# Two edits at the start of a fused attention and MLP kernel: which PSUM bank a score tile takes, and where the decay rows stand among the first loads

## The chip, the cores and the metric

The kernel runs on one core of one Trainium2 chip. The metric is the device time of one execution in microseconds. Three runs of the kernel before gave 341.88, 343.52 and 344.49 us (median 343.52). A profiled execution took 342.17 us, of which 340.5 us are the span that the profile shows; every time from the profile is counted from the start of that span.

## What is computed

Attention with a forget gate for 8 batches of 8 heads (sequence 576, head size 64), then an MLP over all 4608 tokens with an activation h - tanh(h):

```python
scores = scale * np.matmul(q, k.transpose(0, 1, 3, 2))
cum = np.cumsum(np.log(np.clip(f, 0.0001, 1.0)), axis=-1)
decay = cum[:, :, :, None] - cum[:, :, None, :]
scores = np.where(causal, -1000000000.0, scores + decay)
scores = scores - np.max(scores, axis=-1, keepdims=True)
attn = np.exp(scores)
attn = attn / (np.sum(attn, axis=-1, keepdims=True) + 1e-09)
x = np.matmul(attn, v)      # then tokens x 512
h = x @ w_in                # 512 -> 2048
out = (h - np.tanh(h)) @ w_out
```

## The kernel before

**Tiling.** The work is cut into 32 pairs of heads, four per batch; pair p is batch p // 4, heads 2c and 2c + 1 with c = p % 4. "Slot" in the change's short title is such a pair of batch 0, by its c. The scores of a pair are computed transposed (keys on partitions) in seven tiles (`TILES`, L337): three for each head, and between them tile 3 (`LAST`), which holds the last 64 keys of both heads and is only 128 columns wide. `scores` (L342) multiplies a tile on TensorE into a PSUM bank `ps` (L357), and ScalarE takes the exponential into SBUF (L366). In batch 0 the causal mask is a second matmul into the same bank (L360); from batch 1 on GpSimd masks after the exponential (L376). `values` (L387) multiplies with v into `av` (L394), and VectorE divides (L403 to L405).

**Decay.** It enters the matmul as three extra rows below the 64 of head size: rows `chi` and `clo` (high and low part of the cumulated logarithm) in KT, and `cq` in QT. For pair 0 these rows are computed in place (KS, QS). For the other heads of batch 0 they are copied by three small DMAs on GpSimd's queue, in `bulk` (L218, L220, L221); for later batches by SyncE (`load_aug`, L207). `chi`, `cq` and `clo` are ready at different times: `cq` from ScalarE (L583), `clo` from VectorE (L590).

**Transposes.** In the first two batches q and k come in with the sequence on partitions and are transposed by TensorE (`trans`, L303) and copied to QT and KT by VectorE or ScalarE (L314, L316). While pairs 0 to 3 run (`early`), the transposes go to the three banks `m0` to `m2`; from pair 4 on to the one bank of `ps_tr`. That bank also takes the unread warm-up matmuls of `unread` (L570) and, in batch 0, a third of the score tiles; the others alternate between the two banks of `ps_sc`. A bank is written again only when its last reader, the exponential, is through.

**Order.** All five engines run in the order in which the program is written (`manual_schedule`). `att_items` (L605) lists a pair's steps: scores of a tile, loads that go out at this tile (`LOADS`), transposes of the next pair, values of the pair before, and `turn` (L412), which turns an attention result into columns of XR, the MLP's input. From pair 4 on, steps of the MLP (`mlp1` L456, `mlp2_plain` L497, `mlp2` L521) are laid between them.

**Loads.** All loads from float32 inputs to float16 tiles are issued by GpSimd, one after the other; each of its loads waits until the load eight places ahead of it has landed. The order at the start is: q and k of heads 0 to 3 of batch 0, v for heads 0 and 1, then `bulk`: q and k of heads 4 to 7, the decay rows, v for heads 2 to 7 in four blocks (L131); then q and k of batch 1 in pieces, `win` in two halves (L226), four memsets (`last`, L600 to L603), v of batch 1, `wout` in two halves (L230), and q and k of batch 2 in one load of 576 KB each (L102).

Of the kernel before, what the change touches and what calls it, by code (L numbers as in the profile page):

```python
# [21 lines left out]
def kernel(  # L22
# [13 lines left out]
    B, H, S, D = q.shape  # L36
# [56 lines left out]
    qn, kn = ([t[0:S // NT6, :].rearrange("p (h n d) -> p h n d", h=H, n=NT6) for t in raw] for raw in (qraw, kraw))  # L93
# [7 lines left out]
    def load_qk(dst, src, b, h0, h1):  # L101
        nc.gpsimd.dma_start(  # L102
            out=dst[b % 2][:, h0:h1, :, :].rearrange("p h n d -> p h (n d)"),
            in_=src[b, h0:h1, :, :].rearrange("h (p n) d -> p h (n d)", n=NT6))
# [25 lines left out]
    def load_v_block(b, n, h0, h1):  # L130
        nc.gpsimd.dma_start(out=vn[b % 2][:, n, h0:h1, 0:D],  # L131
                            in_=v[b, h0:h1, n * P:(n + 1) * P, :].rearrange("h p d -> p h d"))
# [68 lines left out]
    def aug_rows(b):  # L201
        i, hs = b % 2, slice(b * H, (b + 1) * H)
        return [(KT[i][D:D + 1, :, 0:S], chi[hs, :]), (KT[i][D + 1:D + 2, :, 0:S], clo[hs, :]), (QT[i][D + 2:D + 3, :, :], cq[hs, :])]
# [10 lines left out]

    def bulk():
        (k_hi, chi_0), (k_lo, clo_0), (q_hi, cq_0) = aug_rows(0)
        load_qk(qn, q, 0, 4, H)
        nc.gpsimd.dma_start(out=k_hi, in_=chi_0)  # L218
        load_qk(kn, k, 0, 4, H)
        nc.gpsimd.dma_start(out=q_hi, in_=cq_0)  # L220
        nc.gpsimd.dma_start(out=k_lo, in_=clo_0)  # L221
        for n in range(NJ - 1):
            load_v_block(0, n, 2, H)

# [101 lines left out]
    def head_tiles(a):  # L326
        return [[(a, 0, 0, 512, 0)],
                [(a, 1, P, 448, 0), (a, 0, 512, 64, 448)],
                [(a, 2, 2 * P, 320, 0), (a, 3, 3 * P, 192, 320)]]
# [7 lines left out]
    TILES = head_tiles(0) + [[(0, 4, 512, 64, 64), (1, 4, 512, 64, 128)]] + head_tiles(1)  # L337
    LAST = 3
# [1 line left out]
             4: (0, 1, 1, P), 5: (0, 1, 1, P), 6: (0, 2, 320, P)}  # L340

    def scores(b, c, ti):  # L342
        if b == 0 and (((c - 1) * len(TILES) + ti) % 3 == 2 if c else ti == LAST):
            ps = ps_tr.tile([P, UW], FP32, tag="tr", name="ps")
        else:
            ps = ps_sc.tile([P, 512], FP32, tag="sc", name="ps")
        if ti == LAST:
            e = EL[(b * NPAIR + c) % 3]
        else:
            e = aex.tile([P, 512], FP16, tag="e", name="e")  # L350
        lo = min(x[4] for x in TILES[ti])
        hi = max(x[4] + x[3] for x in TILES[ti])
        kt, qt, rows = (KS, QS, NX) if b == 0 and c == 0 else (KT[b % 2], QT[b % 2], D + 3)
        for a, j, i0, n, col in TILES[ti]:
            h = 2 * c + a
            cut = min(P, n) if b == 0 and i0 == j * P else 0
            nc.tensor.matmul(out=ps[:, col:col + n], lhsT=kt[0:rows, h, j * P:(j + 1) * P],  # L357
                             rhs=qt[0:rows, h, i0:i0 + n], start=True, stop=cut == 0)
            if cut:
                nc.tensor.matmul(out=ps[:, col:col + cut], lhsT=id16, rhs=late[:, 0:cut],  # L360
                                 start=False, stop=True)
            for ib in range(j, NJ):
                w0 = min(ib * P, S - P)
                if i0 <= ib * P < i0 + n:
                    E[(b, c, a, j, ib)] = e[:, col + w0 - i0:col + w0 - i0 + P]
        nc.scalar.activation(out=e[:, lo:hi], in_=ps[:, lo:hi], func=AF.Exp, scale=qscale)  # L366
        if b == 0:
            return
        col, cp, step, wd = MASKS[ti]
        view = e[:, col:col + (cp - 1) * step + wd]  # L370
        if cp == 1:
            pat = [[1, wd]]
        else:
            view = bass.AP(view.tensor, view.offset, [list(view.ap[0]), [step, cp], [1, wd]])
            pat = [[0, cp], [1, wd]]
        nc.gpsimd.affine_select(out=view, in_=view, compare_op=ALU.is_ge, fill=0.0,  # L376
                                base=0, pattern=pat, channel_multiplier=-1)
# [198 lines left out]
    def start():  # L576
        def row_q(h, mul, add):
            nc.scalar.activation(out=QS[NH:NX, h, :], in_=cum[NH:NX, :], func=AF.Identity, bias=add[NH:NX, :], scale=mul[NH:NX, :])

        unread(47)  # L580
        row_q(0, mul_0, add_0)
        q_rest = trans(*pairs[0], qn, (QS,), True, "AAAA", True)
        nc.scalar.activation(out=cq, in_=cum[0:NH, :], func=AF.Copy, bias=-SHIFT * inv_qscale, scale=inv_qscale)  # L583
        unread(6)
        k_rest = trans(*pairs[0], kn, (KS,), True, "VVVV", True)
        unread(38)
        q_rest[0]()
        scores(*pairs[0], 0)
        unread(4)
        nc.vector.scalar_tensor_tensor(out=clo, in0=cum[0:NH, :], scalar=inv_qscale, in1=chi[0:NH, :], op0=ALU.mult, op1=ALU.subtract)  # L590
        nc.vector.tensor_copy(out=KS[NH:NX, 1, 0:S], in_=KS[NH:NX, 0, 0:S])
        for fn in k_rest:
            fn()
        scores(*pairs[0], 1)
        row_q(1, mul_1, add_1)
        unread(4)
        q_rest[1]()
# [7 lines left out]
    def att_items(p):  # L605
# [8 lines left out]
        for ti in range(len(TILES)):  # L614
            if here and (p > 0 or ti > 1):
                put(scores, *here, ti)
# [47 lines left out]
    at = 0  # L664
    start()
    bulk()
    for p in range(len(pairs) + 1):
        b, c = divmod(p, NPAIR)
# [54 lines left out]
```

## Time and profile before

| | |
|---|---|
| median of three runs | 343.52 us |
| profiled execution | 342.17 us |
| its span | 340.5 us |
| TensorE busy | 330.9 us, 97 % of the span |
| VectorE, ScalarE, GpSimd busy | 262.5, 235.1, 162.7 us |
| transfers issued by GpSimd | 18.39 MB, 92512 packets |

The page's second part cuts the span into 40 slices of 8.5 us; each digit is the busy share of an engine in tenths, and the last two rows give the mean busy share of the 16 DMA engines and what they moved:

```profile
PE   8798999999999999999999999999999999999995
DVE  8898887658887788677967886688668766966864
ACT  6897777888887886778677877787558842632630
POOL 8884846686657673776377547632322210000000
DMA  9999999999989999999999999990130023002003
GB/s 117 143 179 200 192 201 171 171 144 163 135 98 120 188 137 101 132 172 121 106 125 165 137 101 95 192 134 16 50 113 16 19 58 103 0 33 92 1 15 110
```

TensorE (PE) is full nearly everywhere; its gaps lie in the first slices and after its last matmul. The first slices hold batch 0, in which no MLP work fills the gaps yet. A busy share hides short waits, so the stretches, the waits and the order of single instructions must be read as well.

In the views that follow, a line gives start, length, engine, source line, operation, output and inputs; a bracket gives the idle time before it and what ended that. A "landing" is the time from the issue of a load to its end.

### The profile page before, as it was taken

The page shows a single profiled execution, that of the slowest core. Times are in us where ns is not written, and L with a number is a line of the kernel's source. Part 1 is how long each engine was busy: PE and PEld are TensorE (multiplying, and loading weights), DVE is VectorE, ACT ScalarE, POOL GpSimd, SP SyncE. Part 2 cuts the span into 40 slices and gives each one's busy share as a digit, 9 for nine tenths or more (in the row PEclk, how much of TensorE's full clock was granted, in tenths as well). Part 3 has the DMA queues.
Part 4 walks back from the last instruction along what each step waited for, and adds up shares of the span by engine and source line. Part 5 has one row for each costly group of instructions (what it writes and reads, how often), then busy time and mean ns, then how long its engine had stood idle before and what let it go on. Part 6 is the DMA issues. An engine that isn't in the chain of part 4 may idle for free.

```text
span 340.5 us, 8626 instructions
## 1 busy us (share of the span) xinstructions
PE 330.9 (97%) x3255; PEld 229.6 (67%) x3255; DVE 262.5 (77%) x516; ACT 235.1 (69%) x440; POOL 162.7 (48%) x321
## 2 busy tenths in 40 slices
PE   8798999999999999999999999999999999999995
PEld 7675555555588458855788888656875686486485
DVE  8898887658887788677967886688668766966864
ACT  6897777888887886778677877787558842632630
POOL 8884846686657673776377547632322210000000
PEclk9999999999999999999999999999999999999999
DMA  9999999999989999999999999990130023002003
GB/s 117 143 179 200 192 201 171 171 144 163 135 98 120 188 137 101 132 172 121 106 125 165 137 101 95 192 134 16 50 113 16 19 58 103 0 33 92 1 15 110
DMA packets 144941, 38.86 MB, mean 114 GB/s; under 512 B 128188, under 2 KB 143276, under 8 KB 144900
## 3 DMA queue, kind: packets, MB, share of 16 engines
q0 software_dynamic: 92512, 18.39, 72.9%
q1 hardware_dynamic: 52356, 19.88, 32.3%
q8 instruction: 25, 0.41, 0.5%
q14 instruction: 16, 0.13, 0.1%
q10 hardware_dynamic: 32, 0.06, 0.0%
HBM read 36.90 MB, written 9.44 MB: 136 GB/s over the span
## 4 chain that ended last, share of the span: by engine, by line
PE 82%; DMA 10%; POOL 6%; issue 1%; ACT 1%; DVE 0%; POOLq 0%
PE hps L456 33%; PE ops L521 29%; PE ps L357 10%; PE av L394 7%; DMA kn<-in_k_dram 6%; DMA win<-in_moe_w_in_dram 4%; PE ops L497 3%; POOL qn L102 1%; POOL vn L131 1%; POOL kn L102 1%; POOL vn L127 1%; PE t L303 1%; POOL vn L123 0%; ACT KT L314 0%; POOL win L226 0%
## 5 line engine op out<-in xcount | busy, mean ns | idle before, releaser
L456 PE MATMUL hps<-XR,win 128*128 128x512 f16 (+1 forms) x640 | 141.0, 357 | 0.3 <-ACT XR L426 0.2
L461 ACT ACTIVATE th<-hps 128x512 f32<-128x512 f32 x144 | 86.7, 602 | 55.2 <-PE hps L456 52.4
L467 DVE TENSOR_TENSOR gq<-hps,th 128x512 f16<-128x512 f32 x144 | 98.3, 688 | 25.0 <-ACT th L461 23.5
L366 ACT ACTIVATE e<-ps 128x512 f16<-128x512 f32 x192 | 110.3, 597 | 10.0 <-PE ps L357 6.6
L376 POOL TENSOR_SCALAR_AFFINE_SELECT e<-e 128x128 f16<-128x128 f16 x168 | 60.5, 362 | 69.5 <-ACT e L366 67.1
L456 PEld LDWEIGHTS <-win 128*128 128x128 f16 x640 | 57.7, 97 | 48.7 <-issue 0.7
L357 PE MATMUL ps<-QT,KT 67*128 67x512 f16 (+1 forms) x372 | 73.6, 276 | 1.8 <-DMA KT<-clo 1.0
L521 PEld LDWEIGHTS <-gq 128*128 128x128 f16 x640 | 60.3, 97 | 11.1
L521 PE MATMUL ops<-wout,gq 128*128 128x256 f16 x512 | 63.2, 272 | 0.0
L357 PEld LDWEIGHTS <-KT 67*128 67x128 f16 x372 | 35.3, 98 | 25.1 <-DVE KT L316 1.9
L394 PEld LDWEIGHTS <-e 128*128 128x128 f16 x896 | 32.3, 97 | 4.2
L394 PE MATMUL av<-vn,e 128*128 128x65 f16 x896 | 33.6, 193 | 0.0
L131 POOL DMA_DIRECT2D vn<-in_v_dram x32 | 28.0, 877 | 8.1 <-DMA win<-in_moe_w_in_dram 3.0
L521 PE MATMUL ops<-W,sq 128*128 128x256 f16 x256 | 31.2, 272 | 0.0
L405 DVE TENSOR_TENSOR xn<-av,rs 128x640 f16<-128x640 f32 x32 | 26.4, 825 | 1.1
L521 PEld LDWEIGHTS <-sq 128*128 128x128 f16 x256 | 24.1, 97 | 3.4
L376 POOL TENSOR_SCALAR_AFFINE_SELECT el<-el 128x128 f16<-128x128 f16 x28 | 9.3, 332 | 28.4 <-ACT el L366 28.0
L108 POOL DMA_DIRECT2D kn<-in_k_dram x25 | 21.2, 847 | 1.5 <-issue 1.3
L108 POOL DMA_DIRECT2D qn<-in_q_dram x25 | 21.2, 847 | 1.3 <-issue 0.9
L403 DVE TENSOR_SCALAR rs<-av 128x10 f32<-128x10 f32 x32 | 5.2, 162 | 18.9 <-PE av L394 17.8
L536 ACT ACTIVATE m<-ops 128x512 f32<-128x512 f32 x16 | 9.5, 596 | 10.9 <-PE ops L521 10.9
L316 DVE COPY QT<-t 64x576 f16<-64x576 f16 x18 | 14.4, 802 | 2.9 <-PE t L303 2.8
(93 smaller groups left out, 314.4 us busy)
## 6 DMA issues: line engine op xcount, KB each, us to landing
out_dram<-ost SPq DMA_DIRECT2D x34, 256.0 KB
vn<-in_v_dram POOLq DMA_DIRECT2D x24, 128.0 KB, 6.1
qn<-in_q_dram POOLq DMA_DIRECT2D x20, 128.0 KB, 5.0
kn<-in_k_dram POOLq DMA_DIRECT2D x20, 128.0 KB, 4.5
win<-in_moe_w_in_dram POOLq DMA_DIRECT2D x2, 1024.0 KB, 12.2
wout<-in_moe_w_out_dram POOLq DMA_DIRECT2D x2, 1024.0 KB, 14.6
XR<-xn SPq DMA_TRANSPOSE x56
vn<-in_v_dram POOLq DMA_DIRECT2D x12, 64.0 KB, 5.5
```

The lines of the kernel that those rows point to most:

```text
L108: nc.gpsimd.dma_start(out=dst[b % 2][0:pn, n, :].rearrange("p (h d) -> p h d", h=H), in_=src[b, :, n * P:n * P + pn, :].rearrange("h p d - ...
L131: nc.gpsimd.dma_start(out=vn[b % 2][:, n, h0:h1, 0:D], in_=v[b, h0:h1, n * P:(n + 1) * P, :].rearrange("h p d -> p h d"))
L316: nc.vector.tensor_copy(out=to, in_=of)
L357: nc.tensor.matmul(out=ps[:, col:col + n], lhsT=kt[0:rows, h, j * P:(j + 1) * P], rhs=qt[0:rows, h, i0:i0 + n], start=True, stop=cut == 0)
L366: nc.scalar.activation(out=e[:, lo:hi], in_=ps[:, lo:hi], func=AF.Exp, scale=qscale)
L376: nc.gpsimd.affine_select(out=view, in_=view, compare_op=ALU.is_ge, fill=0.0, base=0, pattern=pat, channel_multiplier=-1)
L394: nc.tensor.matmul(out=av[:, a, ib, :], lhsT=E.pop((b, c, a, j, ib)), rhs=vn[b % 2][:, j, 2 * c + a, 0:D + 1], start=(j == 0), stop=(j == ib))
L405: nc.vector.tensor_tensor(out=xn.rearrange("p i (a d) -> p a i d", a=2), in0=av[:, :, :, 0:D], in1=rs.to_broadcast([P, 2, NJ, D]), op=ALU. ...
L456: nc.tensor.matmul(out=hps[:, o:o + n], lhsT=win[:, ci, ft * P:(ft + 1) * P], rhs=XR[:, ci, t:t + n], start=(ci == 0), stop=(ci == NCH - 1))
L461: nc.scalar.activation(out=th, in_=hps, func=AF.Tanh, scale=-1.0)
L467: nc.vector.tensor_tensor(out=GQ[(u, i)][:, half, kt, :], in0=hps, in1=th, op=ALU.add)
L521: nc.tensor.matmul(out=ps[:, m, :], lhsT=LHS[lhs](u, kt // 4)[:, kt % 4, m * P:(m + 1) * P], rhs=rhs[:, kt, :], start=(fresh and (apart or ...
```

## The change

The first hunk reorders `bulk`. Before, q of heads 4 to 7 is one load, then the chi row, then k of heads 4 to 7 as one load, then the cq and the clo row. Afterwards q and k of heads 4 and 5 go out first, then the three rows, then q and k of heads 6 and 7; the blocks of v follow as before. The bytes are the same; two loads of 288 KB become four of 144 KB.

The second hunk changes which score tiles of pairs 1 to 3 of batch 0 take the transposes' bank: those whose running number (7 (c - 1) + tile) leaves the remainder 0 instead of 2 when divided by 3. Pair 1 had tiles 2 and 5 there and now has 0, 3 and 6; pair 2 had 1 and 4 and now has 2 and 5; pair 3 had 0, 3 and 6 and now has 1 and 4. Pair 0 (tile 3) is unchanged. The other tiles take the two banks of `ps_sc` in turn, and the order of instructions on TensorE, VectorE, ScalarE and SyncE stays the same.

```diff
     def bulk():
         (k_hi, chi_0), (k_lo, clo_0), (q_hi, cq_0) = aug_rows(0)
-        load_qk(qn, q, 0, 4, H)
+        load_qk(qn, q, 0, 4, 6)
+        load_qk(kn, k, 0, 4, 6)
         nc.gpsimd.dma_start(out=k_hi, in_=chi_0)
-        load_qk(kn, k, 0, 4, H)
         nc.gpsimd.dma_start(out=q_hi, in_=cq_0)
         nc.gpsimd.dma_start(out=k_lo, in_=clo_0)
+        load_qk(qn, q, 0, 6, H)
+        load_qk(kn, k, 0, 6, H)
         for n in range(NJ - 1):
             load_v_block(0, n, 2, H)
...
     def scores(b, c, ti):
-        if b == 0 and (((c - 1) * len(TILES) + ti) % 3 == 2 if c else ti == LAST):
+        if b == 0 and (((c - 1) * len(TILES) + ti) % 3 == 0 if c else ti == LAST):
             ps = ps_tr.tile([P, UW], FP32, tag="tr", name="ps")
```

## The prediction

> **What bounds the kernel now.** I read four views in this order: busy time by stretch, the chain of waits, TensorE's own idle times, then GpSimd's queue beside VectorE's. The first says where time can change at all (columns: stretch, its length, then busy us of TensorE, weight loads, VectorE, ScalarE, GpSimd, the clock, the DMA share, GB/s):
>
> ```profile
> 8.50:17.00 8.50, 6.46 (x97) 5.13 (x94) 6.85 (x12) 7.33 (x14) 7.33 (x12) 1.00 1.46 142
> 17.00:34.00 17.00, 15.42 (x247) 11.20 (x244) 15.53 (x28) 14.59 (x30) 11.34 (x19) 1.00 1.26 190
> 34.00:57.00 23.00, 22.12 (x195) 12.03 (x194) 20.01 (x33) 18.07 (x35) 14.88 (x31) 1.00 1.50 192
> 60.00:300.00 240.00, 239.96 (x2319) 166.01 (x2318) 183.79 (x361) 174.65 (x330) 119.53 (x243) 1.00 1.13 110
> ```
>
> From 60 to 300 us TensorE is busy for 239.96 of 240.00, and the change touches none of its work there. So the end moves by as much as TensorE's entry into that full stretch moves. Before 57 us it has 2.04 + 1.58 + 0.88 = 4.5 us of idle time: that caps any gain. The chain that ended last passes through this:
>
> ```profile
> 14.97 0.65 POOL kn L102
> 15.62 0.63 POOL qn L102
> 16.25 0.62 POOL kn L102
> 16.87 0.76 POOL win L226
> ...
> 21.17 1.46 POOL vn L127 x2
> 22.64 14.40 DMA win<-in_moe_w_in_dram
> ...
> 37.33 19.14 DMA kn<-in_k_dram
> ```
>
> Read it as: GpSimd issues without a pause, then the stream of its transfers carries the chain to 56.47, where k of batch 2 lands. TensorE's idle list names what waits for it:
>
> ```profile
> 15.20 0.38 PE L357 MATMUL ps<-QT,KT 67*128 67x512 f16 x1 [0.98 <-DMA KT<-clo]
> ...
> 28.08 0.41 PE L303 MATMUL t<-id,qn 96*128 96x96 f16 x6 [0.68 <-ACT e L366]
> ```
> ```profile
> 56.51 0.43 PE L303 MATMUL t<-id,kn 96*128 96x96 f16 x6 [0.58 <-DMA kn<-in_k_dram]
> ```
>
> The first two waits are what the two edits touch. The third is a gate behind both: TensorE was ready at 55.93, and the transposes of pair 8's k start when the transfer has landed. Whatever is won earlier is handed back there unless that transfer lands earlier too.
>
> **Edit 1, the decay rows.** GpSimd's queue around it (start, length; a bracket is idle time and what ended it):
>
> ```profile
> 8.06 0.71 POOL L102 DMA_DIRECT2D kn<-in_k_dram  x1
> 9.42 0.52 POOL L220 DMA_DIRECT2D QT<-cq  x1 [0.65 <-DMA kn<-in_k_dram]
> 10.17 0.52 POOL L221 DMA_DIRECT2D KT<-clo  x1 [0.23 <-DVE clo L590]
> 10.68 2.52 POOL L131 DMA_DIRECT2D vn<-in_v_dram  x3
> 13.46 0.83 POOL L131 DMA_DIRECT2D vn<-in_v_dram  x1 [0.26 <-DMA qn<-in_q_dram]
> 14.28 0.66 POOL L102 DMA_DIRECT2D qn<-in_q_dram  x1
> ```
>
> Gain side. The clo row goes out at 10.17 and took 4.8 us to land (14.97): ahead of it in the stream lie 288 KB of q (landed 13.1) and 288 KB of k (landed 14.7). Its issue can't move, since clo itself is ready at 9.88, but 144 KB of each now lies behind it. The q, k loads of 144 KB at 14.28 and 14.97 took 3.7 and 3.8 us with little ahead of them, so I put the row's landing between 13.5 and 14.2. Next late is VectorE:
>
> ```profile
> 12.85 1.61 DVE L316 COPY KT<-t 64x576 f16<-64x576 f16 x2
> 15.93 1.64 DVE L316 COPY QT<-t 64x576 f16<-64x576 f16 x2 [1.46 <-PE t L303]
> ```
>
> The KT copies end at 14.46, so the scores of pair 1 start near 14.57 rather than 15.20: 0.63 us earlier. From 15.93 to 28.37 VectorE is busy nearly without a gap and TensorE waits for it (0.55 us at 19.25), so the whole run of pairs 1 to 3 moves up by these 0.63 us. What it then needs earlier is there: heads 4, 5 are needed by 15.47 and now land at about 12 and 13.
>
> Cost side. Two loads of 288 KB become four of 144 KB. Issuing one costs 0.63 to 0.71 us at 144 KB and 0.67 to 0.71 at 288 KB: GpSimd pays by the load, not by the byte. So 2 x 0.65 = 1.3 us are added. Up to 10.7 the order costs nothing: the two first loads end at about 8.2, the chi row at 8.7, and cq and clo are still issued at 9.42 and 10.17, when their inputs are ready. The loads of heads 6, 7 come at 10.7 and 11.4, and the four blocks of v start at 12.0 rather than 10.68. The 0.26 us wait before the fourth block falls away: it waits for the transfer eight places ahead (the program gives GpSimd eight in flight), which is now a 144 KB load, down by about 12. Net shift of everything GpSimd issues from 14.28 on: 1.3 - 0.26 = about 1.05 us. That is loads for batch 1, `win`, the memsets of `last` and, through the eight places, all that follows: the second block of v of batch 1 waited to 27.22 for `win`, k of batch 2 to 37.33 for the second half of `win`.
>
> Does that delay reach the landings? The fourth block of v landed 3.8 us after its issue, the next two loads 3.7 and 3.8. The shortest landing of any q, k or v load in the trace is 3.5 us, so the stream was nearly empty at 14 to 16 us and landings followed issues. From 21 to 54 us it moves 156 to 221 GB/s and the eight places fill: a steady backlog, in which a late start stays late up to k of batch 2. Its bounds: 0 if the stream makes the delay good (17 to 21 us ran at 118 to 181 GB/s, and 20 % of spare rate over 4 us is about 0.8 us), 1.5 us if all issues cost the 0.83 us of the slowest one. I take 1.0, nearest to the landings of 3.7 and 3.8 us.
>
> The covers of that delay: `win` landed at 26.96 and is first used at 29.73, which moves up to about 28.9; at 28.0 it still holds with 0.9 us left. Masks of pair 4 on GpSimd end at 36.9, then 37.9; their reader starts at 39.0, then 38.3. EL[2]'s memset ends at 19.85, then 20.9, against 22.03, then 21.4. Each cover, gone, would cost the excess alone, and all lie ahead of the gate at 56 us, so they add nothing below 1 us.
>
> A rule speaks against splitting: the Trainium skill (DMA: Bandwidth & Descriptors, Anatomy of one DMA) gives each load issued by GpSimd a fixed 2.0 us beside its bytes. By it the two extra loads would add 4 us, if loads did not overlap. The trace has landings of 144 KB loads 0.7 to 1.5 us apart, so they overlap, and the sum does without it.
>
> **Edit 2, the banks.** No instruction is added or moved; only which bank a score tile takes. Inside pairs 1 to 3 a bank comes back after three tiles before and after. At 28.08 TensorE waits 0.68 us for the exponential of pair 3's tile 6, which sits in the transposes' bank; afterwards that bank was last used by tile 4 (its exponential ends at 26.86). The price: tile 0 of pair 4 now waits for tile 5 (27.54) instead of tile 4 (26.86), so it starts about 0.5 us later than 27.02. The transposes then start near 27.85 instead of 28.08. But their copies on VectorE queue behind the division, which ends at 28.37; they began at 28.53 after waiting 0.16 us. So 0.16 us is all that VectorE can use, and turning pair 2 needs that division anyway. Bounds 0 and 0.23; taken 0.16.
>
> **Sum.** TensorE reaches the gate 0.63 + 0.16 = 0.79 us earlier, at about 55.1; k of batch 2 lands 1.0 us later, at about 57.5. The gate's idle time grows from 0.58 to about 2.4 us and the end moves by +1.0: 343.2 against the profiled execution's 342.17 (its span is 340.5). That execution lies 1.35 us below the median of the runs shown; against the median the forecast is 343.52 + 1.0 = 344.5.
>
> **Rivals.** *The stream absorbs the delay.* k lands at 56.5 as before and the front gain turns into idle time at the gate: 343.5. For it: the slow rates at 18 to 19 us. Against: the 3.7 us landings.
>
> *The gate isn't the limit.* If k lands early enough, the gain shows, at most min(0.79 + 0.58, 4.5) = 1.4 us: 342.1. For it: the runs spread over 2.6 us, so landings may vary. Against: no byte is saved ahead of k. Going below 340.1 would take 3.4 of 4.5 idle us; no row offers it.
>
> *Slower: loads that don't overlap.* A load of 144 KB landing in 3.7 us spends 0.66 on issue and about 0.7 on its bytes, leaving 2.3 fixed. If the stream paid that for each of two more loads, k would land 4.6 us later: 348.1. It decides once the two loads of heads 6, 7 land over 2 us apart. Against: four blocks of v landed 0.4 to 0.8 us apart.
>
> *Slower: the clock.* The first 47 warm-up matmuls took 4.24 us (90 ns each), 38 later ones 2.29 (60 ns each): TensorE starts slow. If 2.4 us of waiting at the gate puts it back, a second warm-up costs 47 x 0.03 = 1.4 us more: 345.9. Against: gaps of 0.86, 0.15 and 0.98 us within 11.3 to 15.2 left the 512-column matmuls at 17.19 at full rate (the next start 0.22 us later).
>
> **How the numbers follow.** Forecast 0.55, absorbed 0.15, gate not the limit 0.09, loads that don't overlap 0.13, clock 0.08. Within 1 % (340.1 to 347.0) is about what a measurement of this kernel can't tell from no change. The forecast's own range is 343.5 to 345.0 by the bounds of the delay, with a run spread of 1 to 1.5 us around it. Faster by over 1 %: 0.05, from the second rival and the spread. Slower by over 1 %: 0.19, from the third, half the clock case and a tail of the forecast. The rest, 0.76, within. Range 341.8 to 347.4: it takes in all but the loads that don't overlap and the outer tails.
>
> **What would show it.** Right: the wait for clo at 15.2 gone, pair 1's scores at 14.6; the fourth block of v issued near 14.6; `win` landing near 28; no wait of the transposes for the exponential at 28; a wait of over 1.5 us for k near 57. Wrong: k of batch 2 landing at 56.5 or before, or a wait after 60 us.

## The result, and the profile after

The changed kernel took 345.62 us (median of 19 runs, 342.45 to 347.25), the kernel before 342.58 us (19 runs, 341.41 to 344.87): a ratio of 1.0077, with a 95 % interval of 1.0051 to 1.0102. By that ratio, which is the ratio of the means, it is slower by 2.6 us (the medians lie 3.0 us apart), where +1.0 was forecast. A run that took over 1.5 % more than the fastest of its kernel is left out of such comparisons, which is why some experiments below compare 11 runs of 12.

The profiled execution took 342.45 us, with a span of 340.7 us against 340.5 before. That is almost no loss, and it is the first thing to notice: this execution isn't typical of the changed kernel. Each run lists the mean clock that TensorE was granted. The profiled run had 1.000; two others had it too (342.66 and 343.49 us). The remaining 16 runs had 0.988 to 0.995 and took 344.9 to 347.3 us. So there are two questions: what the trace at full clock shows, and what the other runs lost.

At full clock, busy time by stretch after the change (the columns are those of the prediction):

```profile
8.50:17.00 8.50, 7.11 (x112) 5.62 (x109) 7.50 (x13) 8.00 (x16) 7.53 (x12) 1.00 1.30 127
17.00:34.00 17.00, 15.63 (x237) 11.12 (x234) 15.48 (x28) 14.91 (x30) 12.23 (x21) 1.00 1.28 187
34.00:57.00 23.00, 20.99 (x185) 11.20 (x184) 19.37 (x31) 17.15 (x33) 15.09 (x32) 1.00 1.45 195
60.00:300.00 240.00, 239.95 (x2319) 165.98 (x2318) 183.90 (x361) 175.05 (x331) 120.20 (x243) 1.00 1.11 111
```

TensorE does 0.65 us more by 17 us, and has 1.1 us more of idle time from 34 to 57 us: won in front, handed back at the gate. Its idle list shows both:

```profile
14.51 0.39 PE L359 MATMUL ps<-QT,KT 67*128 67x512 f16 x1 [0.30 <-DVE KT L318]
...
26.91 0.38 PE L359 MATMUL ps<-QT,KT 67*128 67x512 f16 x1 [0.41 <-ACT e L368]
...
53.92 0.43 PE L305 MATMUL t<-id,qn 96*128 96x96 f16 x6 [0.47 <-DMA qn<-in_q_dram]
56.95 0.43 PE L305 MATMUL t<-id,kn 96*128 96x96 f16 x6 [1.29 <-DMA kn<-in_k_dram]
```

The wait for the clo row is gone, and VectorE's copies are next late; the transposes at 28 us no longer wait, but tile 0 of pair 4 now does; and at the gate there are 1.76 us of waiting instead of 0.58. GpSimd's queue:

```profile
9.45 0.53 POOL L220 DMA_DIRECT2D QT<-cq  x1 [0.79 <-ACT cq L585]
10.15 0.51 POOL L221 DMA_DIRECT2D KT<-clo  x1 [0.18 <-issue]
10.66 0.66 POOL L102 DMA_DIRECT2D qn<-in_q_dram  x1
11.31 0.66 POOL L102 DMA_DIRECT2D kn<-in_k_dram  x1
11.94 3.34 POOL L131 DMA_DIRECT2D vn<-in_v_dram  x4
15.23 0.70 POOL L102 DMA_DIRECT2D qn<-in_q_dram  x1
```

The blocks of v start at 11.94 instead of 10.68, and the load after them at 15.23 instead of 14.28.

### The profile page after: what moved, and what is told of

The parts are those of the page before. It is cut to its first block, busy times and chain, and to the rows that moved or that the text cites. A ratio compares the mean times of both kernels' runs of the same rounds, so it can differ in the third digit from the quotient of the medians.

```text
span 340.7 us, 8628 instructions
## 1 busy us (share of the span) xinstructions
PE 330.9 (97%) x3255; PEld 229.6 (67%) x3255; DVE 262.5 (77%) x516; ACT 235.1 (69%) x440; POOL 163.9 (48%) x323
## 4 chain that ended last, share of the span: by engine, by line
PE 82%; DMA 10%; POOL 4%; DVE 2%; issue 1%; ACT 1%; POOLq 0%
PE hps L458 33%; PE ops L523 29%; PE ps L359 10%; PE av L396 7%; DMA kn<-in_k_dram 6%; DMA win<-in_moe_w_in_dram 4%; PE ops L499 3%; POOL vn L131 1%; POOL qn L102 1%; POOL kn L102 1%; PE t L305 1%; POOL vn L127 0%; DVE TQ L195 0%; ACT KT L316 0%; DVE W L198 0%
## 5 line engine op out<-in xcount | busy, mean ns | idle before, releaser
L378 POOL TENSOR_SCALAR_AFFINE_SELECT el<-el 128x128 f16<-128x128 f16 x28 | 9.3, 330 | 28.7 <-ACT el L368 28.2
L405 DVE TENSOR_SCALAR rs<-av 128x10 f32<-128x10 f32 x32 | 5.2, 163 | 18.9 <-PE av L396 17.8
L491 DVE TENSOR_TENSOR gq<-gq 128x512 f16<-128x512 f16 x32 | 16.6, 518 | 0.0
```

The source lines that it names most:

```text
L491: nc.vector.tensor_tensor(out=LHS[name](u, i)[:, ks], in0=LHS[x](u, i)[:, ks], in1=LHS[y](u, i)[:, ks], op=op)
```

## The experiments

Times are medians. In each group the kernel before ran beside the others on the same chip; it took 342.63, 342.43, 342.37 and 342.44 us. "Clock kept" means a mean granted clock of 0.998 or more. The kernel before loses its clock in part of its runs too: in the first group 18 of the 34 runs compared kept it (median 341.9 us) and 16 did not (343.4 us). So a kernel whose runs all keep the clock is to be compared with 341.9 us.

**The changed kernel again.** No edit.

> The changed kernel once more, for its spread and a second trace. The profiled execution of it took 342.45 us at a granted clock of 1.000, but 16 of its 19 runs took 344.9 to 347.3 us at a mean clock of 0.988 to 0.995. Theory A (clock): the longer wait for q and k of batch 2 near 54 to 57 us makes TensorE lose its clock for some microseconds in most executions. Then most runs here take 345 to 347 us with a mean clock under 1, and a trace of such a run shows matmuls at half rate for 4 to 8 us beginning near that wait. Theory B (landing): in the usual execution k of batch 2 lands 2 to 3 us later than in the profiled one, and the clock is a side effect. Then a trace of a usual run shows k landing at 59 to 60 us.

345.22 us, ratio 1.0045 (1.0015 to 1.0075). Of the 11 runs compared, four kept the clock (median 342.5 us); seven had 0.994 or 0.995 (median 345.35 us). This time the trace is of one of the seven. Two stretches of it, TensorE's clock in the third column from the right:

```profile
58.50:61.90 3.40, 3.40 (x40) 2.28 (x38) 0.80 (x1) 0.60 (x1) 0.85 (x1) 0.50 3.02 143
62.00:66.00 4.00, 4.00 (x34) 2.19 (x32) 3.27 (x7) 3.04 (x5) 2.68 (x5) 1.00 2.04 172
```
```profile
54.53 0.43 PE L305 MATMUL t<-id,qn 96*128 96x96 f16 x6 [1.20 <-DMA qn<-in_q_dram]
58.23 0.43 PE L305 MATMUL t<-id,kn 96*128 96x96 f16 x6 [1.96 <-DMA kn<-in_k_dram]
```
```profile
58.49 1.88 PE L499 MATMUL ops<-wout,gq 128*128 128x512 f16 x4
...
61.93 1.03 PE L499 MATMUL ops<-wout,gq 128*128 128x512 f16 x4
```

Both theories have a part in it. k landed 1.3 us later than in the first trace (58.2 against 56.9), so TensorE waited 3.16 us in all. Right after that it ran for 3.4 us at half its clock: four 512-column matmuls took 1.88 us there and 1.03 us afterwards. Work that takes 3.4 us at half the clock takes 1.7 us at full clock, so 1.7 us are lost. 1.3 + 1.7 = 3.0; the two spans differ by 343.6 - 340.7 = 2.9 us.

**One hunk at a time.** Only the order of the loads (the changed kernel with the banks as before):

```diff
-        if b == 0 and (((c - 1) * len(TILES) + ti) % 3 == 0 if c else ti == LAST):
+        if b == 0 and (((c - 1) * len(TILES) + ti) % 3 == 2 if c else ti == LAST):
```

> Only the first hunk (order and size of the loads); the banks as before. The wait for the clo row is gone, the wait of the transposes for the exponential at 28 us is back, so TensorE reaches the gate about 0.15 us later than with both hunks. Theory A: the wait at the gate is still over 1.5 us in all, so the clock is still lost in most runs: 344.5 to 346.5 us. Theory B: the load stream is that of the changed kernel, so 345.5 us, like it.

344.74 us, ratio 1.0042 (1.0009 to 1.0075), as the changed kernel. Its trace waits 0.51 and 1.58 us at the gate; five of the 11 runs compared kept the clock. Only the banks (the kernel before with the new banks):

```diff
-        if b == 0 and (((c - 1) * len(TILES) + ti) % 3 == 2 if c else ti == LAST):
+        if b == 0 and (((c - 1) * len(TILES) + ti) % 3 == 0 if c else ti == LAST):
```

> Only the second hunk (banks); loads as before. TensorE reaches the gate 0.1 to 0.2 us earlier than before and k lands as before. Theory A: the wait at the gate grows from 0.58 to about 0.75 us; the clock is lost in a few runs more than before at most: 342.5 to 343.5 us. Theory B: 342.6 us, no change.

341.94 us, ratio 0.9985 (0.9962 to 1.0007): not to be told from no change. The loss shows with the first hunk alone. Five of the 12 runs of this kernel lost the clock, and its trace is of one of them. The clock fell at 14.9 us, right behind the wait for the clo row, and no wait for k was left at the gate (k landed at 55.3):

```profile
14.92:18.34 3.42, 3.42 (x41) 2.95 (x40) 2.43 (x4) 1.79 (x3) 3.42 (x6) 0.50 1.44 154
```

That run took 341.45 us, no more than the runs that kept the clock (median 341.9 us). The waits of 0.55 us at 19 us and of 0.58 us at the gate, which the kernel before has, are gone from its trace, and k happened to land early. So a drop ahead of the gate can disappear in idle time that was there anyway. The drop behind the gate has none to disappear in: from 60 us on TensorE is full.

**Work in the wait.** The changed kernel, with unread matmuls in front of the two transposes that wait at the gate:

```diff
         else:
             t32 = ps_tr.tile([P, UW], FP32, tag="tr", name="t32")
+        if (b, c) == (2, 0):
+            for i in range(20 if src is kn else 8):
+                nc.tensor.matmul(out=t32[:, i % 4 * P:i % 4 * P + P], lhsT=warm, rhs=warm, start=True, stop=True)
```

> The changed kernel with 28 unread 128-column matmuls more: 8 ahead of the transposes of q and 20 ahead of the transposes of k of pair 8, into the banks that these transposes fill next, so that TensorE is at work while it waits for q and k of batch 2 (28 x 0.056 = 1.6 us). They save no waiting. Theory A: the clock stays at 1.000 in nearly all runs and the time falls to 342.5 to 343.5 us. Theory B: 345.5 us as without them, or up to 0.5 us more.

343.62 us, ratio 1.0030 (1.0008 to 1.0052). All 12 runs kept the clock (0.998 to 1.000). In the trace the unread matmuls take 0.61 us ahead of q and 1.28 us ahead of k, and both waits still end with the landing (0.56 and 0.68 us of idle time are left), so they delayed nothing. k is still late:

```profile
58.06 0.43 PE L308 MATMUL t<-id,kn 96*128 96x96 f16 x6 [0.68 <-DMA kn<-in_k_dram]
```

So the idle time in this wait is what costs the clock, and keeping it gives back 1.7 us: the runs of the changed kernel that lost the clock had a median of 345.35 us. That is half of a 3.4 us stretch. What remains is the late landing. Against all runs of the kernel before it is 1.0 us, but that median includes runs that lost their clock; against those that kept it, it is 343.6 - 341.9 = 1.7 us. k landed at 58.0 here, 1.5 us later than in the trace of the kernel before.

**Why k lands late.** First, two issues without bytes. The kernel before, with two tiny loads ahead of the blocks of v:

```diff
+    spare = cst.tile([H, 2, S // 4], FP16)
+
     def bulk():
...
         nc.gpsimd.dma_start(out=k_lo, in_=clo_0)
+        nc.gpsimd.dma_start(out=spare[:, 0, :], in_=chi[0:H, 0:S // 4])
+        nc.gpsimd.dma_start(out=spare[:, 1, :], in_=chi[0:H, 0:S // 4])
```

> The kernel before with two tiny loads more (8 x 144 halves of the chi rows into a tile that nobody reads) between the clo row and the blocks of v: about 1.0 us more of GpSimd's issue time there, 0.75 after the wait of 0.26 us that falls away, nearly no bytes, the order of everything else as before. Theory A1: k of batch 2 lands about 0.75 us later, the wait at the gate grows from 0.58 to about 1.3 us, median 343.4 us with the clock kept and up to 345 us where it is lost. Theory A2: 342.6 us, no change.

343.44 us, ratio 1.0050 (1.0015 to 1.0084); five of 12 runs kept the clock (342.9 us), the others took 345.0. The trace waits 0.72 us for q and 0.97 us for k, which lands at 57.4. Two issues of 0.5 us, with next to no bytes and nothing reordered, cost about as much as the change. They add more than their issue time, though: two more loads also shift the eight places, and the second block of v now waits 0.53 us, where the fourth waited 0.26 us before. So of the 1.2 us by which the load behind the blocks comes later (15.48 against 14.28), 1.0 is issue time and the rest is that wait; the two were not separated.

```profile
13.04 2.47 POOL L131 DMA_DIRECT2D vn<-in_v_dram  x3 [0.53 <-DMA qn<-in_q_dram]
```

Second, two issues fewer, but behind the blocks of v. The changed kernel, with this edit (q and k of heads 0 to 3 of batch 1 in one load each):

```diff
-    LOADS = {(0, 1): [lambda: load_qk(qn, q, 1, 0, 2), lambda: load_qk(kn, k, 1, 0, 2)],
-             (0, 4): [lambda: load_qk(qn, q, 1, 2, 4), lambda: load_qk(kn, k, 1, 2, 4)],
+    LOADS = {(0, 1): [lambda: load_qk(qn, q, 1, 0, 4), lambda: load_qk(kn, k, 1, 0, 4)],
```

> The changed kernel with two loads fewer behind the change: q and k of heads 0 to 3 of batch 1 in one load of 288 KB each (at tile 1 of pair 0) instead of two of 144 KB. GpSimd's issues of win and all behind it come 1.3 us earlier than in the changed kernel, 0.2 us earlier than before; same bytes. Theory A1 (GpSimd's time for two more issues delays the stream, so q and k of batch 2 land later, and the longer wait costs the clock): k lands about 1.2 us earlier than in the changed kernel, median 342.0 to 343.0 us, few runs under a clock of 0.996 for a late drop. Theory A2 (the order of the loads or their smaller size makes the stream slower): 344.5 to 345.5 us, as the changed kernel.

346.91 us, ratio 1.0126 (1.0086 to 1.0166). The expectation of 342 to 343 us failed. GpSimd issued `win` at 16.5 instead of 17.8, yet it landed at 28.2, as in the changed kernel (28.1), and k at 57.1. So issuing sooner behind the blocks of v did not bring these landings forward. It did make up bytes: from 18 to 54 us the stream moved 199 GB/s, against 194 in the changed kernel (table below). So the bytes alone do not decide when k lands. Why this kernel lost the clock for longer in most runs (mean clock 0.988 to 0.990 in six of eight; the trace is of a run that kept it) was not seen.

Third, the blocks of v sooner. The changed kernel's banks, the loads of heads 4 to 7 in one piece of q and one of k, and the rows on SyncE:

```diff
+        load_qk(qn, q, 0, 4, H)
+        load_qk(kn, k, 0, 4, H)
         (k_hi, chi_0), (k_lo, clo_0), (q_hi, cq_0) = aug_rows(0)
-        load_qk(qn, q, 0, 4, 6)
-        load_qk(kn, k, 0, 4, 6)
-        nc.gpsimd.dma_start(out=k_hi, in_=chi_0)
-        nc.gpsimd.dma_start(out=q_hi, in_=cq_0)
-        nc.gpsimd.dma_start(out=k_lo, in_=clo_0)
-        load_qk(qn, q, 0, 6, H)
-        load_qk(kn, k, 0, 6, H)
+        nc.sync.dma_start(out=k_hi, in_=chi_0)
+        nc.sync.dma_start(out=q_hi, in_=cq_0)
+        nc.sync.dma_start(out=k_lo, in_=clo_0)
```

> The changed kernel's banks, the loads of heads 4 to 7 in one piece of q and one of k as before, and the three decay rows of batch 0 issued by SyncE instead of GpSimd. GpSimd then issues the four blocks of v from about 8.2 us instead of 10.7 (before) and 11.9 (changed). Theory A3 (the stream runs dry while GpSimd is busy with issues ahead of the blocks of v, and what is lost up to 16 us is not made up): the last of the four blocks lands at 15 to 16 us instead of 17.3 (before) and 18.3 to 18.6 (changed), k of batch 2 lands 1 to 2 us earlier than before, by 55.5 us, and the median falls to 341.0 to 342.0 us. If the place of the four blocks does not matter: k at 56.5 us or later and 342.4 us or more.

342.85 us, ratio 1.0005 (0.9982 to 1.0029). k of batch 2 landed at 54.9, 1.5 us before the kernel before had it, and no wait at the gate is left. The last block of v landed no sooner (18.5), against the expectation; what moved up comes behind it: k of heads 2 and 3 of batch 1 by 0.3 us against the kernel before, `win` by 1.2. But the clo row, now in the other queue, landed late:

```profile
16.09 0.38 PE L357 MATMUL ps<-QT,KT 67*128 67x512 f16 x1 [1.82 <-DMA KT<-clo]
```
```profile
16.50:19.50 3.00, 3.00 (x40) 2.66 (x38) 2.50 (x4) 1.79 (x3) 2.74 (x7) 0.50 1.34 198
```

The same chain as at the gate, at another place: 1.82 us of waiting, then half the clock, for 3.4 us from 16.5; 11 of its 12 runs lost some. The one run that kept its clock took 340.71 us.

Four traces show what the stream moved from 8 to 16 us (last column, GB/s): before, changed, merged loads, rows on SyncE:

```profile
8.00:16.00 8.00, 5.96 (x82) 4.67 (x80) 6.33 (x12) 6.81 (x13) 6.83 (x11) 1.00 1.48 141
```
```profile
8.00:16.00 8.00, 6.61 (x95) 5.24 (x92) 7.00 (x12) 7.48 (x14) 7.03 (x12) 1.00 1.25 127
```
```profile
8.00:16.00 8.00, 6.79 (x100) 5.52 (x98) 6.91 (x11) 7.34 (x14) 7.01 (x12) 1.00 1.22 125
```
```profile
8.00:16.00 8.00, 5.21 (x74) 4.21 (x71) 6.30 (x11) 6.52 (x13) 6.57 (x10) 1.00 1.65 164
```

At 18 us the shortfall is larger still. These are all traces in which k of batch 2 is one load, by what the stream moved up to 18 us and afterwards and by when k landed:

| trace | GB/s, 8 to 18 us | GB/s, 18 to 54 us | k lands, us |
|---|---|---|---|
| kernel before | 147 | 194 | 56.5 |
| only the banks | 152 | 195 | 55.3 |
| rows on SyncE | 168 | 198 | 54.9 |
| changed kernel | 128 | 194 | 56.9 |
| changed kernel again | 124 | 193 | 58.2 |
| only the order of the loads | 132 | 191 | 57.7 |
| work in the wait | 129 | 194 | 58.0 |
| two tiny loads | 125 | 192 | 57.4 |
| merged loads | 122 | 199 | 57.1 |

The changed kernel's 128 instead of 147 GB/s are 190 KB less in 10 us, 1.0 us at 194 GB/s, and the rate afterwards, 191 to 195 GB/s in all but two, does not bring them back. In all six traces with issues added ahead of the blocks of v the early rate is lower and k lands at 56.9 to 58.2; in the other three k lands at 54.9 to 56.5. Within either group landings differ by 1.3 to 1.6 us, and the two executions of the changed kernel alone by 1.3, so a difference of half a microsecond between two traces says nothing. Both of the earliest landings (only the banks, rows on SyncE) are also of executions whose clock had dropped near 15 us; whether that drop helps the loads was not tested, so the 1.5 us of the rows on SyncE aren't shown to come from the rows alone.

**The gate taken away.** First try, on the kernel before and on the changed kernel:

```diff
-            add((p0, 5), load_qk, qn, q, b, 0, H)
-            add((p0, 6), load_qk, kn, k, b, 0, H)
+            add((p0, 5), load_qk, qn, q, b, 0, 2)
+            add((p0, 5), load_qk, kn, k, b, 0, 2)
+            add((p0, 6), load_qk, qn, q, b, 2, H)
+            add((p0, 6), load_qk, kn, k, b, 2, H)
```

> The kernel before with q and k of batch 2 in two loads each: heads 0 and 1 (144 KB each) first, then heads 2 to 7. k of pair 8 then lands at about 52.5 us, ahead of the transposes that need it at 55.9, so the gate is gone. Theory A: the wait of 0.58 us falls away and no late drop of the clock can follow: 341.6 to 342.3 us. If the gate is not what sets the entry into the full stretch: 342.6 us.

> The changed kernel with the same split of q and k of batch 2. Theory A: without the gate the 0.63 + 0.16 us that both hunks win at the front reach the end and the late drop of the clock is gone: about 0.8 us below the kernel before with the same split, 340.8 to 341.7 us. If the front gain is lost elsewhere (a cover behind it, like masks on GpSimd that come 1 us later): 342 us or more.

347.64 us (1.0143, 1.0101 to 1.0184) and 348.32 us (1.0169, 1.0131 to 1.0206). Both expectations failed. k of heads 0 and 1 landed at 52.4 and 52.6 as hoped, but two loads more move the places in the queue: a block of v of batch 2 now waited on GpSimd until `wout`'s second half had landed (51.2), and the masks of pair 5 stood behind it. From the changed kernel's version:

```profile
51.74 0.88 POOL L131 DMA_DIRECT2D vn<-in_v_dram  x1 [4.87 <-DMA wout<-in_moe_w_out_dram]
...
52.98 0.23 PE L398 MATMUL av<-vn,e 128*128 128x65 f16 x2 [4.27 <-POOL e L380]
```
```profile
54.00:57.00 3.00, 2.99 (x24) 1.73 (x25) 0.00 (x0) 0.42 (x2) 1.36 (x5) 0.50 1.75 182
```

4.27 us of waiting, and again half the clock, for 3.4 us; no run of either kernel kept it. Second try: q of heads 0 and 1 at tile 5 of pair 4, the other three loads at tile 6, and the last two blocks of v of batch 2 put off:

```diff
+        if b == 2:
+            at_v = [(5, 0), (5, 1), (5, 4), (6, 5), (6, 6)]
...
-            add((p0, 5), load_qk, qn, q, b, 0, H)
-            add((p0, 6), load_qk, kn, k, b, 0, H)
+            add((p0, 5), load_qk, qn, q, b, 0, 2)
+            add((p0, 6), load_qk, kn, k, b, 0, 2)
+            add((p0, 6), load_qk, qn, q, b, 2, H)
+            add((p0, 6), load_qk, kn, k, b, 2, H)
```

> The changed kernel with q and k of batch 2 split so that heads 0 and 1 come first, and with the last two blocks of v of batch 2 put off to pair 6's tiles 5 and 6. In the first try at this, one of those blocks stood in GpSimd's queue waiting for the second half of wout (it landed at 51.2 us), and the masks of pair 5 waited behind it: TensorE stood 4.3 us. Now no block waits there. Theory A: k of pair 8 lands at 52.5 us, no wait of TensorE over 0.3 us is left between 32 and 60 us, the late drop of the clock is gone in nearly all runs, and the front gain of 0.8 us reaches the end: 341.0 to 342.0 us. If the front gain is lost elsewhere: 342.5 us or more.

340.47 us, ratio 0.9935 (0.9910 to 0.9960): faster than both kernels. All six runs lie between 340.35 and 341.30 us at a clock of 0.999 or 1.000. k of heads 2 to 7 of batch 2 lands at 58.8, later than in any other trace, and nothing waits for it. From 34 to 57 us TensorE is busy nearly throughout:

```profile
34.00:57.00 23.00, 22.77 (x225) 12.97 (x224) 20.29 (x32) 17.83 (x34) 16.53 (x36) 1.00 1.43 195
```

> The kernel before with the same repair as the one that gave 340.47 us with the change: q and k of batch 2 split, the last two blocks of v of batch 2 put off. It tells what both hunks are worth where no gate follows. Theory A (the front gain is real and was only hidden behind the gate): TensorE enters the full stretch 0.8 us later than with the change, 341.2 to 341.5 us in runs at a clock of 1.000; the wait of about 1 us for the clo row is still there, so an early drop of the clock near 15 to 18 us comes in part of the runs and now reaches the end: 342 to 343.5 us there, median 341.3 to 342.5 us. If the hunks are worth nothing at the front: 340.5 us.

The same repair without the change: 341.24 us, ratio 0.9976 (0.9949 to 1.0002). Eight of 12 runs kept the clock (341.1 us), four took 342.5 to 343.5 us at 0.990 to 0.995. So with the gate away the change is worth 0.6 us at full clock by the medians, 0.4 us by the means. The two kernels ran in different groups, so a value this small is only an indication, and none of six runs with a lost clock against four of 12 is too few to tell.

The repair on top of the rows on SyncE:

> Both together: rows on SyncE, banks of the change, and q and k of batch 2 split with the last two blocks of v put off. Theory A: no wait at the gate, front gain kept, no late drop of the clock: 340.8 to 341.6 us, below the kernel before by 0.3 to 0.5 per cent. If a wait of the masks on GpSimd takes over: 342 us or more.

343.54 us, ratio 1.0033 (1.0008 to 1.0057). The clo row was late again (1.76 us), and its trace ran at half clock from about 16 to 22.5 us. With the gate away, no later wait takes that loss up.

## Why the prediction was right, and where its size was off

**The front gain.** Scores of pair 1 at 14.51 (forecast 14.57), with VectorE next late. Right in the profiled execution. In part of the executions the row is in time before the change too: in the trace of the kernel before with the second repair the same scores start at 14.41 and wait only for VectorE. So 0.63 us is the gain of one execution, not of all; 0.4 to 0.6 us for both hunks together, with the gate away, is what the runs indicate for the end.

**Edit 2.** The wait of 0.68 us went, and 0.41 us for tile 5's exponential came in its place (0.5 forecast). TensorE does 0.21 us more from 17 to 34 us (15.63 against 15.42), close to the 0.16 taken. Alone it is worth nothing that could be told from the spread.

**The cost.** The issue after the blocks of v came 0.95 us later (1.05 forecast), `win` landed at 28.1 (28.0), and its cover held. k of batch 2 landed at 56.9 in one trace and 58.2 in the other (57.5), with two more traces of the same loads at 57.7 and 58.0. The path is only half right. In the profiled execution the delay shrank on the way: k waits for the second half of `win`, as forecast, but that landed only 0.18 us later, so k was issued 0.18 us later (before, then after):

```profile
37.33 0.78 POOL L102 DMA_DIRECT2D kn<-in_k_dram  x1 [0.47 <-DMA win<-in_moe_w_in_dram]
```
```profile
37.51 0.78 POOL L102 DMA_DIRECT2D kn<-in_k_dram  x1 [0.56 <-DMA win<-in_moe_w_in_dram]
```

In the second trace k was issued at 37.94 and landed 1.7 us later than before. What the runs show is that issues added ahead of the blocks of v, while the stream runs below its later rate, leave bytes missing, and in five of the six traces these are not made up by 54 us. By which loads this reaches k is left open. The term of 1.0 us was too low: with the clock kept by the work in the wait, the late landing costs 1.7 us against the runs of the kernel before that kept theirs.

**The gate.** Right, and the most useful step: TensorE was ready for q of batch 2 at 53.45 instead of 54.21, and these 0.8 us gave nothing while the gate stood. The wait for k alone was 1.29 us in the first trace and 1.96 in the second, where over 1.5 was named as the sign.

**The step that failed: the clock.** The prediction let the clock stay because gaps of 0.86, 0.15 and 0.98 us before 15.2 us had left the matmuls at 17.19 at full rate. That was one execution that had kept its clock. Among the runs of the kernel before, 16 of 34 compared with the first group had a mean clock under 0.998 (median 343.4 us against 341.9 with it kept), so the trace could not carry that argument. In the changed kernel 16 of 19 runs lost it. The price was also low: 1.4 us from the warm-up matmuls, where one lost stretch costs 1.7 us. An estimate of the +2.6 us from these numbers: 1.7 for the late landing, 1.4 for a lost stretch of 1.7 us in 16 of 19 runs, less 0.7 for what the kernel before loses itself (1.5 us in 16 of 34 runs) make 2.4. So the measured time is the forecast plus this rival, with the cost larger than forecast. That the time of 345.62 us lies so near the rival's 345.9 is partly luck: the forecast started from the median of three runs, 343.52 us, and the median of 19 is 342.58, so the base was 0.9 us too high where the terms were too low.

## What to carry to other kernels

A front gain is worth what the next gate lets through: look for the transfer or wait that everything passes later, and move that first. Price an extra load by the issue time that it takes from the loads behind it, above all where the stream is about to run dry. Before arguing from the clock of one trace, look at the clock of all runs: a wait of 1 to 2 us in a full engine can cost as much again after it.

## What the runs showed of the hardware that was not expected

TensorE's clock dropped to 0.50 for 3.4 us after waits of 1.82 us (rows on SyncE), 3.16 us in two parts (the changed kernel again), 3.87 and 4.27 us (first repair, on either kernel), and once from 14.9 us after 0.86, 0.15 and 0.66 us (only the banks). With the rows on SyncE and the gate away it dropped for 6.8 us, twice as long, around a wait of 1.76 us. It stayed at 1.00 in traces with waits of 1.76 us in two parts (the changed kernel) and 2.09 us in two parts (only the order of the loads). At such lengths it differs from run to run of one kernel; what decides it was not seen. Unread matmuls of 0.61 and 1.28 us in the waits kept it in all of 12 runs.

The clo row, 9 KB, was issued at 10.01 by SyncE and at 10.15 by GpSimd (changed kernel). GpSimd's landed 2.8 us later, behind its own loads; for SyncE's, TensorE waited until 16.09, some 6 us, while GpSimd's stream moved 164 GB/s beside it. A queue of its own did not make it faster here, nor in the second trace with the rows on SyncE, where the same scores began at 15.88.
